# Moving column sums and gate logits into the matrix multiplications, and transposing on chip instead of through DRAM, in a fused forward and backward kernel

## The chip, the cores and the metric

The kernel runs on one core of a Trainium2 chip. The metric is the device time of one execution, in microseconds (us). The engines are named as the profile names them: PE (TensorE, matrix multiplications), PEld (its weight loads), DVE (VectorE), ACT (ScalarE), POOL (GpSimd) and SP (SyncE, which here only issues DMA transfers; "SPq" is its queue). PEclk is the clock that PE was granted, as a share of full speed. Time counts from the start of the profiled span.

A run is fast unless it is over 1.5% above the fastest run of the same kernel.

## The reference

Forward and all gradients of a gated mix of linear attention and an MLP, in bf16, with S = 2048 rows, D = 640, 32 heads of 20, and F = 1728.

```python
x = A_x                                                # (S, D)
g = sigmoid((x * gate_w).sum(-1, keepdims=True))       # one gate per row
q, k, v = split_heads(x @ wqkv)
phi = lambda t: where(t > 0, t + 1, exp(t)) + 1e-6
pq, pk = phi(q), phi(k)
kv  = einsum("bhsd,bhse->bhde", pk, v)                 # per head, over all rows
z   = einsum("bhsd->bhd", pk)                          # column sum of pk
num = einsum("bhqd,bhde->bhqe", pq, kv)
den = einsum("bhqd,bhd->bhq", pq, z)[..., None] + 1e-6
a = merge_heads(num / den) @ wo
b = relu(x @ w1) @ w2
out = g * a + (1 - g) * b       # and the gradients for x, wqkv, wo, w1, w2, gate_w
```

The kernel never forms v for all rows. It computes Y = xᵀ·pk (640 x 640), from it the head blocks KVT = wvᵀ·Y masked to a block diagonal, and from those M = KVT·wo, so that the attention output is pq·M.

## The kernel before

All stages stand in one program. For each of the 16 chunks of 128 rows, the k stage forms `kp = x_chunk @ wk` on PE and turns it into `pk` by a chain: an exponential on ACT, a tensor_scalar on DVE, a maximum on DVE. GpSimd adds every `pk` chunk into `zacc`.

```python
    def phi_chain(ps_flat, dst):
        eb = tmp("tb", 8)
        nc.scalar.activation(eb[:], ps_flat, ACT.Exp)
        cp = tmp("tb", 8)
        nc.vector.tensor_scalar(cp[:], eb[:], 1.0, 1e-6, ALU.min, ALU.add)          # L373
        nc.vector.scalar_tensor_tensor(dst, ps_flat, 1.0 + 1e-6, cp[:], ALU.add, ALU.max)   # L374

    def k_chunk(i):
        kp = pp("kp")
        for k in range(KD):
            mm_cols(kp, xT(i, k), lambda a, e: wk_s[:, k, a:e], k == 0, k == KD - 1)
        phi_chain(flat(kp)[:, 0:D], pkN[:, i, :])
        if i == 1:
            nc.gpsimd.tensor_tensor(zacc, pkN[:, 0, :], pkN[:, 1, :], ALU.add)
        elif i > 1:
            nc.gpsimd.tensor_tensor(zacc, zacc, pkN[:, i, :], ALU.add)              # L418
        ...
    nc.gpsimd.memset(KVT_s, 0.0)                                                    # L444
```

Then Y follows, five blocks of 16 x 2 matmuls. Each block needs all 16 `pk` chunks. Between the blocks stand the 16 gate products on DVE, and the fp32 column sum on PE.

```python
    for m in range(KD):
        yp = pp("yp")
        for i in range(NT):
            mm_cols(yp, xN[:, i, csl(m)], lambda a, e: pkN[:, i, a:e], i == 0, i == NT - 1)
        copy_out(m, Y_s[:, m, :], flat(yp)[:, 0:D])            # ACT for even m, DVE for odd
        for i in range(4 * m, min(4 * m + 4, NT)):
            jk = tmp("tb", 8)
            nc.vector.scalar_tensor_tensor(jk[:], xN[:, i, :], 1.0, gwb[:], ALU.mult, ALU.mult,
                                           accum_out=lg_t[:, i:i + 1])              # L454
        if m == 1:
            zp = pp("zp")
            mm_cols(zp, ones_f[:], lambda a, e: zacc[:, a:e], True, True)
            nc.scalar.copy(zb[:], flat(zp)[:, 0:D])
        ...
    nc.sync.dma_start(Y_d.rearrange("(k p) d -> p k d", p=P), Y_s)
    ...
    q_main(0)
    blockdiag(KVT_s, wv_s, Y_s)
    nc.scalar.dma_start(KVT_d..., KVT_s)
    h_half(0, 0); h_half(0, 1)
    for t in range(KD):
        ...                                                    # MT, five blocks
    nc.scalar.dma_start(MT_d..., MT_s)
    load_T(M_s, MT_d)                                          # M comes back transposed
    q_post(0)
    for i in range(1, NT + LAG):
        ...                                                    # q, h, output chunks
```

Buffers are placed by lifetime in one memory plan. `ar.add(name, bytes, t0, t1)` says from when to when a buffer lives; two buffers whose lifetimes do not overlap may share space. KVT has the lifetime `T_FF - 20` to `T_FF + 30`, so its memset must wait until the buffer whose space it takes has been read for the last time.

The order in which each engine executes is fixed when the program is built, by a scheduler that starts from the order of the code. It can move instructions that do not depend on each other.

## Time and profile before

The median of the first five runs was 652.08 us (651.24 to 652.99). These are lines of the profile's page for the kernel before: the span, the busy time of each engine (with its share of the span and its instructions), and PE's granted clock in 40 equal slices of 16 us, in tenths of full speed.

```profile
span 650.1 us, 10572 instructions
...
PE 639.2 (98%) x4480; PEld 356.8 (55%) x4480; DVE 262.2 (40%) x518; ACT 151.0 (23%) x209; POOL 119.5 (18%) x111
...
PEclk9989999999999999999999999999999999999999
```

PE is the limit: it is busy for 639.2 of 650.1 us. One slice has a lowered clock, the third (32.5 to 48.8 us). The next view names what PE waited for: the waits of PE in the kernel before, with the tile and line that waited, the releaser, and the us in total, times, and longest.

```profile
PE yp L328 <- DVE arena L374: 4.1, 1, 4.1
...
PE kp L328 <- DVE arena L374: 0.6, 1, 0.6
PE op L328 <- DMA arena<-arena: 0.6, 1, 0.6
...
```

The largest wait is one: Y's matmuls waited 4.1 us for the DVE line L374, the maximum that completes `pk`. The timeline of PE in the kernel before shows where (start, us, then engine, line, operation and count; in brackets the idle time before and its releaser).

```profile
30.70 4.24 PE L328 MATMUL yp<-arena 128*128 128x512 bf16 x30
39.01 6.46 PE L328 MATMUL yp<-arena 128*128 128x512 bf16 x34 [4.08 <-DVE arena L374]
45.30 1.30 PE L328 MATMUL zp<-arena,ones_f 128*128 128x512 f32 x4
```

Thirty matmuls ran, which is 15 of the 16 chunks; the last two of the block waited from 34.93 to 39.01. The same moments on DVE and on GpSimd, again from the timeline of the kernel before:

```profile
32.96 3.33 DVE L373 TENSOR_SCALAR tb<-tb 128x640 bf16<-128x640 bf16 x1
36.21 2.00 DVE L454 SCALAR_TENSOR_TENSOR tb<-arena,gwb 128x640 bf16<-128x640 bf16 x1
...
38.15 0.81 DVE L374 SCALAR_TENSOR_TENSOR arena<-kp,tb 128x640 bf16<-128x640 f32 x1
```

```profile
30.53 2.88 POOL L418 TENSOR_TENSOR arena<-arena 128x640 f32<-128x640 f32 x2
33.35 2.76 POOL L444 MEMSET arena<- 128x3200 bf16 x1
36.07 1.46 POOL L418 TENSOR_TENSOR arena<-arena 128x640 f32<-128x640 f32 x1
```

The last tensor_scalar took 3.33 us and ended as GpSimd's memset of KVT ended. Earlier in the k stage each tensor_scalar took 0.63 beside the sums, 0.33 without one, so that a chunk cost DVE 1.48 us and PE only 1.36.

The stall had a second cost. The windows view of the kernel before gives the busy time of PE, PEld, DVE, ACT and POOL in each stretch, then PE's clock, the share of DMA and its GB/s:

```profile
34.90:39.00 4.10, 0.04 (x1) 0.00 (x0) 4.10 (x5) 0.00 (x0) 2.63 (x2) 1.00 1.07 344
39.00:42.50 3.50, 3.49 (x13) 1.64 (x13) 3.50 (x7) 0.69 (x1) 1.84 (x1) 0.51 1.06 388
42.50:46.00 3.50, 3.50 (x24) 2.03 (x23) 3.50 (x9) 0.00 (x0) 0.00 (x0) 1.00 1.06 394
```

After the idle 4.1 us PE had half its clock: 13 matmuls in 3.5 us, then 24 in the next 3.5 us. The first two blocks of Y took 14.6 us in all, two later ones 8.7.

### The profile page before, as it was taken

How to read it: one execution, taken by the hardware profiler on the slowest of the kernel's cores; microseconds unless marked ns; L12 is line 12 of the kernel's file. 1: busy time of each engine (PE TensorE's matmuls, PEld its weight loads, DVE VectorE, ACT ScalarE, POOL GpSimd, SP SyncE). 2: the span in 40 equal slices, each digit the busy share in tenths (PEclk: the TensorE clock that was granted, in tenths of full speed). 3: DMA queues.
4: the chain of work that ended last, by engine and by line, in shares of the span. 5: the costliest groups of instructions: out<-in, count | busy, mean ns of one | idle time of the engine just before them, and what ended most of it. 6: DMA issues, size and time to landing. Idle time of an engine off the chain costs nothing.

```text
span 650.1 us, 10572 instructions
## 1 busy us (share of the span) xinstructions
PE 639.2 (98%) x4480; PEld 356.8 (55%) x4480; DVE 262.2 (40%) x518; ACT 151.0 (23%) x209; POOL 119.5 (18%) x111
## 2 busy tenths in 40 slices
PE   8979999999999999999999999999999999999998
PEld 5546555555555555555555555555555555555554
DVE  4994644554445235566135332220036320004442
ACT  4401322212222123323134343441110111110000
POOL 5840533343333213323001000000000000000000
PEclk9989999999999999999999999999999999999999
DMA  9992994645335893671749999696127539991111
GB/s 270 324 341 92 249 186 93 138 108 109 86 71 118 180 244 93 155 175 71 168 110 240 249 232 241 139 254 159 47 90 149 141 104 266 240 252 41 41 41 41
DMA packets 224889, 103.18 MB, mean 159 GB/s; under 512 B 181579, under 2 KB 224139, under 8 KB 224843
## 3 DMA queue, kind: packets, MB, share of 16 engines
q1 hardware_dynamic: 212874, 87.77, 58.0%
q10 hardware_dynamic: 11968, 14.75, 6.6%
q8 instruction: 35, 0.57, 0.4%
q14 instruction: 12, 0.09, 0.0%
HBM read 27.61 MB, written 29.66 MB: 88 GB/s over the span
## 4 chain that ended last, share of the span: by engine, by line
PE 90%; DVE 5%; DMA 2%; issue 1%; SPq 1%; ACT 1%; POOL 0%; DVEq 0%; ACTq 0%
PE op L328 11%; PE dxp L328 9%; PE gp L705 9%; PE w1p L792 9%; PE w2p L328 9%; PE dp L328 9%; PE hp L516 7%; PE rp L328 3%; PE wkp L328 3%; PE dkp L328 3%; PE qp L328 3%; PE yp L328 3%; PE xp L688 3%; PE wqp L880 3%; DVE tb L373 2%; DVE arena L374 2%
## 5 line engine op out<-in xcount | busy, mean ns | idle before, releaser
L328 PEld LDWEIGHTS <-arena 128*128 128x128 bf16 x2818 | 218.6, 98 | 175.4 <-issue 9.2
L328 PE MATMUL op<-arena 128*128 128x512 bf16 x576 | 80.9, 299 | 0.7 <-DMA arena<-arena 0.6
L516 PE MATMUL hp<-arena 128*128 128x432 bf16 x320 | 62.0, 346 | 0.0
L328 PE MATMUL dxp<-arena 128*128 128x512 bf16 x450 | 61.5, 299 | 0.0
L705 PE MATMUL gp<-arena 128*128 128x432 bf16 x320 | 60.9, 346 | 0.0
L792 PE MATMUL w1p<-arena 128*128 128x432 bf16 x320 | 60.1, 346 | 0.0
L328 PE MATMUL dp<-arena 128*128 128x512 bf16 (+1 forms) x416 | 59.6, 299 | 0.0
L328 PE MATMUL w2p<-arena 128*128 128x512 bf16 (+1 forms) x416 | 59.3, 299 | 0.0
L712 DVE TENSOR_TENSOR arena<-tb,tb 128x864 bf16<-128x864 bf16 x32 | 19.4, 607 | 65.8 <-ACT tb L709 65.7
L792 PEld LDWEIGHTS <-arena 128*128 128x128 bf16 x320 | 30.8, 98 | 26.9 <-issue 0.5
L705 PEld LDWEIGHTS <-arena 128*128 128x128 bf16 x320 | 30.5, 98 | 26.7 <-issue 1.3
L516 PEld LDWEIGHTS <-arena 128*128 128x128 bf16 x320 | 30.4, 98 | 25.8
L484 POOL TENSOR_TENSOR f<-tb,zb 128x640 f32<-128x640 bf16 x16 | 23.4, 1465 | 84.8 <-DVE tb L374 61.7
L709 ACT ACTIVATE tb<-gp,omg_t 128x864 bf16<-128x864 f32 x32 | 31.4, 981 | 32.3 <-PE gp L705 32.3
L552 DVE SCALAR_TENSOR_TENSOR tb<-op,arena 128x640 bf16<-128x640 f32 x16 | 13.2, 824 | 46.4 <-ACT arena L550 46.4
L607 POOL TENSOR_TENSOR f<-zb,grd 128x640 f32<-128x640 bf16 x16 | 20.3, 1272 | 59.4 <-DVE grd L605 59.4
L550 ACT CAST arena<-op 128x640 bf16<-128x640 f32 x16 | 11.1, 692 | 82.4 <-PE op L530 48.9
L893 DVE SCALAR_TENSOR_TENSOR f<-gwb,dl_t,arena 128x640 f32<-128x640 bf16 x16 | 14.0, 884 | 35.9 <-DMA arena<-dxB_d 35.5
L328 PE MATMUL yp<-arena 128*128 128x512 bf16 (+1 forms) x160 | 24.1, 313 | 4.1 <-DVE arena L374 4.1
L903 DVE TENSOR_TENSOR arena<-dxp,f 128x640 bf16<-128x640 f32 x15 | 12.4, 824 | 37.0 <-PE dxp L328 37.0
L373 DVE TENSOR_SCALAR tb<-tb 128x640 bf16<-128x640 bf16 x32 | 18.5, 579 | 18.8 <-ACT tb L371 18.8
L795 ACT CAST arena<-w1p 128x864 bf16<-128x864 f32 x10 | 8.8, 879 | 72.5 <-PE w1p L792 72.5
(129 smaller groups left out, 678.7 us busy)
## 6 DMA issues: line engine op xcount, KB each, us to landing
out_dram<-arena ACTq DMA_DIRECT2D x28, 160.0 KB, 3.9
pk_d<-arena SPq DMA_DIRECT2D x4, 640.0 KB, 9.5
arena<-in_grad_out_dram SPq DMA_DIRECT2D x4, 640.0 KB, 5.3
e_d<-arena SPq DMA_DIRECT2D x8, 320.0 KB, 3.5
out_dram<-arena ACTq DMA_DIRECT2D x8, 320.0 KB, 2.6
arena<-e_d SPq DMA_DIRECT2D x8, 320.0 KB, 3.7
dq_d<-arena SPq DMA_DIRECT2D x8, 320.0 KB, 4.1
dxB_d<-arena ACTq DMA_DIRECT2D x8, 320.0 KB, 3.6
```

Source lines behind the costliest of these rows:

```text
L328: mm = nc.tensor.matmul(ps_tile[:, b, 0:e - a], lhsT=lhsT, rhs=rhs_fn(a, e), start=start, stop=stop, **kw)
L373: nc.vector.tensor_scalar(cp[:], eb[:], 1.0, 1e-6, ALU.min, ALU.add)
L484: nc.gpsimd.tensor_tensor(tz[:], pq[:], zb[:], ALU.mult)
L516: nc.tensor.matmul(hp[:, nb, 0:NBW], lhsT=xT(i, k), rhs=w1_s[:, k, blk * NBW:(blk + 1) * NBW], start=(k == 0), stop=(k == KD - 1))
L607: nc.gpsimd.tensor_tensor(heads(wz[:]), heads(zb[:]), hb(w32[:]), ALU.mult)
L688: nc.tensor.matmul(xp[:, 0, :], lhsT=lhsT, rhs=doX(i)[:, 0:512], start=(i == 0), stop=(i == NT - 1))
L705: nc.tensor.matmul(gp[:, nb, 0:NBW], lhsT=doTg[i // G][:, k, gsl(i)], rhs=w2T_s[:, k, blk * NBW:(blk + 1) * NBW], start=(k == 0), stop=(k ...
L709: nc.scalar.activation(gs[:], gp[:, :, 0:NBW], ACT.Copy, scale=omg_t[:, i:i + 1])
L712: nc.vector.tensor_tensor(hs(i)[:, rng], msk[:], gs[:].rearrange("p b c -> p (b c)"), ALU.mult)
L792: nc.tensor.matmul(wp[:, nb, 0:NBW], lhsT=xN2[:, i, csl(m)], rhs=hs(i)[:, blk * NBW:(blk + 1) * NBW], start=(i == 0), stop=(i == NT - 1))
L880: nc.tensor.matmul(wp[:, 0, :], lhsT=lhsT, rhs=dqN[:, i, 0:512], start=(i == 0), stop=(i == NT - 1))
L893: nc.vector.scalar_tensor_tensor(base[:], gwb[:], dl_t[:, i:i + 1], dxB[:, i, :], ALU.mult, ALU.add)
```

## The change

Its intent is to take work off DVE and GpSimd in the k stage, to fill the end of that stage with other work of PE, and to replace trips through DRAM by transposes from on-chip memory to on-chip memory. It has eight parts:

1. The GpSimd sums `zacc` go. A column of ones is appended to x, so that each Y block (now computed as pkᵀ·x) also yields its part of the column sum z.
2. The 16 gate products on DVE go. gate_w is appended to wk as a column, so the k stage yields the logits, with one small exponential per chunk on ACT.
3. Y is computed transposed, copied by ACT, and transposed by DMA block by block. M comes back by five small transposes. The store of MT to DRAM and the transposed reloads of Y and MT from there go.
4. One of four groups of x is transposed on PE instead of two; the others come by transposing DMA.
5. The q projections of chunks 0 and 1 stand between the k stage and Y.
6. The lifetime of KVT starts at 0, so its memset need not wait.
7. Loads are reordered: gate ahead of wk, wq ahead of wv, grad_out after the first half of h(0).
8. After Y, the halves of h(0) and h(1) stand around the column sum, the block diagonal and M. For the backward pass, Y is stored to DRAM as it was computed (transposed) and loaded back plainly.

The diff, cut to its core:

```diff
-    ar.add("zacc", D * 4, 0, T_FF - 5)
-    ar.add("KVT", KD * D * B2, T_FF - 20, T_FF + 30)
+    ar.add("KVT", KD * D * B2, 0, T_FF + 30)
-    XPE = 2
+    XPE = 1
 ...
+    nc.scalar.dma_start(grow[:], gate_w.rearrange("(k p) -> k p", p=P))
     (loads of wk)
+    nc.gpsimd.memset(xN[:, :, D:D + 1], 1.0)
+    nc.tensor.transpose(gtp0[:, 0, 0:KD], grow[:], ident[:KD, :KD])
+    nc.scalar.copy(wk_s[:, :, D:D + 1], gtp0[:, 0, 0:KD].unsqueeze(2))
 ...
     def k_chunk(i):
-            mm_cols(kp, xT(i, k), lambda a, e: wk_s[:, k, a:e], k == 0, k == KD - 1)
+            mm_cols(kp, xT(i, k), lambda a, e: wk_s[:, k, a:e], k == 0, k == KD - 1, spl=DSP1)
         phi_chain(flat(kp)[:, 0:D], pkN[:, i, :])
-        if i == 1:
-            nc.gpsimd.tensor_tensor(zacc, pkN[:, 0, :], pkN[:, 1, :], ALU.add)
-        elif i > 1:
-            nc.gpsimd.tensor_tensor(zacc, zacc, pkN[:, i, :], ALU.add)
+        nc.scalar.activation(rg_t[:, i:i + 1], flat(kp)[:, D:D + 1], ACT.Exp, scale=-1.0)
 ...
+    q_main(0)
+    q_main(1)
     for m in range(KD):
         yp = pp("yp")
         for i in range(NT):
-            mm_cols(yp, xN[:, i, csl(m)], lambda a, e: pkN[:, i, a:e], i == 0, i == NT - 1)
-        copy_out(m, Y_s[:, m, :], flat(yp)[:, 0:D])
-        for i in range(4 * m, min(4 * m + 4, NT)):
-            ...gate product on VectorE...
-        if m == 1:
-            mm_cols(zp, ones_f[:], lambda a, e: zacc[:, a:e], True, True)
+            mm_cols(yp, pkN[:, i, csl(m)], lambda a, e: xN[:, i, a:e], i == 0, i == NT - 1, spl=DSP1)
+        nc.scalar.copy(YT0_s[:, m, :], flat(yp)[:, 0:D])
+        nc.vector.tensor_copy(zc_t[:, m:m + 1], flat(yp)[:, D:D + 1])
+        nc.vector.tensor_scalar(zd[:, csl(m)], ident[:], zc_t[:, m:m + 1], None, ALU.mult)
+        load_T(Y_s[:, :, csl(m)], YT0_s[:, m, :])
-    nc.sync.dma_start(Y_d..., Y_s)
+    h_half(0, 0)
+    mm_cols(zp, ones_sq[:], lambda a, e: zd[:, a:e], True, True)
+    q_den(0); q_den(1)
+    h_half(0, 1)
     blockdiag(KVT_s, wv_s, Y_s)
+    q_post(0)
+    h_half(1, 0)
     for t in range(KD):
         ...
         copy_out(t, MT_s[:, t, :], flat(mp)[:, 0:D])
-    nc.scalar.dma_start(MT_d..., MT_s)
-    load_T(M_s, MT_d)
+        load_T(M_s[:, :, csl(t)], MT_s[:, t, :])
+    h_half(1, 1)
+    q_post(1)
```

## The prediction

> **What bounds it now.** TensorE: the page shows PE busy 639.2 of 650.1 us. By the waits view its idle time lies in the first 90 us: 1.3 (first memset), 0.7 (x landing), 0.6 and 4.1 (VectorE, k stage), 0.25 and 0.6+0.3 (near the first output chunk). Later it never waits, and no later matmul is removed.
>
> **The k stage and Y.** In the PE timeline a k chunk costs 1.36 us, but VectorE needs 1.48: 0.82 for the maximum, 0.63 for the tensor_scalar, which takes 0.33 where GpSimd rests. The slow ones coincide with the 1.4 us GpSimd sums (zacc); one took 3.3 us beside the GpSimd memset of KVT. [...] Y stops for 4.08 us at its last row block, and the clock record then shows 0.5 for 3.4 us (39.1 to 42.5) [...]. The first two Y blocks take 14.6 us where two others take 8.7.
>
> **What the change removes (estimates from these durations).**
> - stall and cold clock: 14.6 - 8.7 = 5.9 us; VectorE should need about 1.2 per chunk, and two q chunks (2 x 1.36) cover its tail;
> - kp slip: 110 matmuls took 15.75, ideal 15.0: 0.75 us;
> - four of eight x transposes on PE, 0.28 each: 1.1 us;
> - the fp32 column sum (1.13) becomes bf16 (0.27): 0.85 us;
> - the DRAM round trips of Y and M. SP waited 2.2 us for MT's store, with h(1)'s transpose behind it; the first output chunks lost 1.5 us against their later pace: 1.0 to 1.5 us, if the five small transposes (1.2 us of issue each) do not block instead;
> - 16 gate products on VectorE (0.81 each): off the path, 0.
>
> Sum 9.6 to 10.1.
>
> **What it adds.** One column in 160 matmuls (under 0.1 us); a gate load ahead of wk (0.3 to 0.5 at the start); an exponential of about 0.2 per chunk on ScalarE, which has 0.65 spare. x groups 1 to 3 now come by transpose: the two of before moved 1.3 MB in about 7.3 us, so three land by about 9, 13, 17 us, needed at 13, 18, 24; wq by 24, needed at 29. The last Y block must be copied (0.7) and transposed (2.6 to 4.6) before blockdiag; PE has h(0) and the column sum, 3.9 us, to cover it: 0 to 1.5 of stall. The KVT memset moves earlier: up to 0.5. grad_out is issued behind two stores: covered by spare PSUM.
>
> Net gain 8.3 us, nearly all on the critical path: 652.1 - 8.3 = 643.8 us, 8 in 10 between 641.0 and 648.0. Faster by over 2% (below 639.0) 0.04, within 2% 0.94, slower 0.02.
>
> **What would show it.** Right: no PE wait on VectorE before Y, no 0.5 in the clock record after 5 us, kp at 1.36 per chunk, Y ending near 54 us instead of 60, the first output chunk near 71 instead of 79.5, everything later shifted as a block. Wrong: a PE wait on DMA at kp of chunk 4 or 8, at qp, or at blockdiag.
>
> **What would make it wrong.** Transposes slower than estimated among 2 MB of copies; the in-order SP queue blocked [...], so that Y's transposes start late; the scheduler placing memsets or q's phi ahead of the last k's phi.

## The result and the profile after

The kernel after took 644.56 us in the median (8 runs, 644.01 to 644.87), the kernel before beside it 652.6 us (15 runs, 651.24 to 653.93). The ratio is 0.9879, with a 95% interval of 0.9869 to 0.9889. Ratios here are the mean time of one kernel's fast runs over that of the other's of the same rounds, so not quite the ratio of the medians quoted. The gain is 8.0 us; 8.3 were predicted, and 643.8 us with a range of 641.0 to 648.0.

The same lines of the page, for the kernel after:

```profile
span 643.0 us, 10523 instructions
...
PE 636.9 (99%) x4459; PEld 355.4 (55%) x4459; DVE 240.4 (37%) x491; ACT 153.2 (24%) x225; POOL 97.9 (15%) x97
...
PEclk9999999999999999999999999999999999999999
```

The dent in the third slice is gone. PE's waits in the kernel after:

```profile
PE warm L392 <- DVE arena L379: 1.3, 1, 1.3
PE hp L507 <- DVE arena L336: 0.8, 1, 0.8
PE mtp L352 <- DVE arena L368: 0.4, 1, 0.4
PE kp L329 <- DMA arena<-in_A_wqkv_dram: 0.4, 1, 0.4
PE op L523 <- DMA arena<-arena: 0.3, 1, 0.3
```

The wait of Y is gone, and there are two new waits on DVE, 0.8 and 0.4 us, that the kernel before did not have. The timeline of DVE at the end of the k stage, kernel after:

```profile
30.72 0.33 DVE L374 TENSOR_SCALAR tb<-tb 128x640 bf16<-128x640 bf16 x1
31.15 0.82 DVE L375 SCALAR_TENSOR_TENSOR arena<-kp,tb 128x640 bf16<-128x640 f32 x1
```

This last tensor_scalar takes 0.33 us, and the last maximum ends at 31.97, before Y starts at 32.44. The timeline of PE, kernel after:

```profile
29.72 2.88 PE L329 MATMUL qp<-arena 128*128 128x512 bf16 x20
32.44 13.24 PE L329 MATMUL yp<-arena 128*128 128x512 bf16 x96
46.02 8.89 PE L329 MATMUL yp<-arena 128*128 128x512 bf16 x64
...
62.63 2.42 PE L352 MATMUL mtp<-arena 128*128 128x140 bf16 x35 [0.41 <-DVE arena L368]
65.83 1.99 PE L507 MATMUL hp<-arena 128*128 128x432 bf16 x10 [0.77 <-DVE arena L336]
```

Y runs through. The small waits come after it, at M and at h(1). PE's timelines give a full account of the 7.1 us between the two profiled spans (each figure is a difference of start times of two stages):

| stretch of PE | before, us | after, us | difference | predicted |
|---|---|---|---|---|
| start to the end of the k stage | 30.70 | 29.72 | -0.98 | -1.35 to -1.55 |
| Y without the column sum | 28.16 | 22.31 | -5.85 | -5.9 |
| column sum | 1.13 | 0.27 | -0.86 | -0.85 |
| Y to q(3), without q(0), q(1) and the column sum | 23.07 | 23.64 | +0.57 | -1.0 to -1.5 |

From q(3) on, at 85.78 us before and 78.66 after, the two kernels do the same in the same time. The timed gain is 0.9 us larger than that of the profiles, because a profile is one execution. The one of before took 652.17 us, less than that kernel's mean; the one of after took 644.83, more than its mean. The profile of before had one stretch at half clock; by their mean clocks most other runs of that kernel had two (the table under e3).

### The profile page after: what moved, and what is told of

Its sections match the earlier page's. It is cut to its first block, busy times and chain, and to the rows that moved or that the text cites. A ratio compares the mean times of both kernels' runs of the same rounds, so it can differ in the third digit from the quotient of the medians.

```text
span 643.0 us, 10523 instructions
## 1 busy us (share of the span) xinstructions
PE 636.9 (99%) x4459; PEld 355.4 (55%) x4459; DVE 240.4 (37%) x491; ACT 153.2 (24%) x225; POOL 97.9 (15%) x97
## 4 chain that ended last, share of the span: by engine, by line
PE 91%; issue 4%; DMA 2%; DVE 1%; ACT 1%; POOL 0%; ACTq 0%; POOLq 0%; DVEq 0%
PE op L329 11%; PE dxp L329 10%; PE gp L729 9%; PE w1p L816 9%; PE w2p L329 9%; PE dp L329 9%; PE hp L507 8%; PE rp L329 3%; PE wkp L329 3%; PE dkp L329 3%; PE kp L329 3%; PE qp L329 3%; PE xp L712 3%; PE wqp L904 3%; DMA arena<-in_A_wqkv_dram 1%
## 5 line engine op out<-in xcount | busy, mean ns | idle before, releaser
L800 DVE TENSOR_TENSOR tb<-dkp,dzb 128x640 bf16<-128x640 f32 x16 | 13.1, 819 | 62.5 <-PE dkp L329 62.5
L329 PE MATMUL rp<-arena 128*128 128x512 bf16 (+1 forms) x160 | 24.4, 299 | 0.0
L482 POOL TENSOR_TENSOR arena<-tb,grd 128x640 bf16<-128x640 bf16 x16 | 20.3, 1271 | 25.9 <-DVE grd L476 23.7
```

Source lines behind the costliest of these rows:

```text
L329: mm = nc.tensor.matmul(ps_tile[:, b, 0:e - a], lhsT=lhsT, rhs=rhs_fn(a, e), start=start, stop=stop, **kw)
L482: nc.gpsimd.tensor_tensor(heads(pg), heads(pq[:]), hb(grd[:]), ALU.mult)
```

## The experiments

Twelve kernels ran. This is what the letters in the expectations stand for.

- A: the stall is made at the very end of DVE's queue, by the memset beside the last tensor_scalar and by the gate product ahead of the last maximum.
- B: the stall is made by the slow pace of DVE through the whole k stage, which is due to the GpSimd sums. This is what the prediction held.
- C: the two q chunks ahead of Y are the cover that removes it.
- D: in the new kernel it is the early place of the memset that counts.

The twelve ran in three batches, each on one chip, with runs of the kernel before beside them: medians 652.78 (e), 652.29 (f) and 652.72 (g).

| run | base | edit | median us | ratio to before | correct |
|---|---|---|---|---|---|
| e1 | before | KVT's lifetime from 0 | 646.29 | 0.9903 | yes |
| e2 | before | no sums | 646.75 | 0.991 | no |
| e3 | before | no gate products | 649.1 | 0.9943 | no |
| e4 | before | q(0), q(1) ahead of Y | 657.07 | 1.0049 | yes |
| g4 | before | e1 and e3 together | 644.52 | 0.9873 | no |
| f1 | after | q(0), q(1) behind Y | 644.09 | 0.987 | yes |
| f2 | after | the sums put back, unused | 645.5 | 0.9894 | yes |
| f3 | after | KVT's lifetime as before | 644.44 | 0.9878 | yes, edit had no effect |
| g1 | after | the memset held back | 644.4 | 0.9869 | yes |
| g3 | after | masks ahead of reductions | 644.09 | 0.9875 | yes |
| f4 | after | waits after Y removed | 642.53 | 0.9846 | yes |
| g2 | f4 | gate load behind wk | 645.46 | 0.9889 | yes |

### e1: the memset early, in the kernel before

```diff
-    ar.add("KVT", KD * D * B2, T_FF - 20, T_FF + 30)
+    ar.add("KVT", KD * D * B2, 0, T_FF + 30)
```

> The kernel before with one edit: the buffer KVT may be cleared from the start, so GpSimd's 2.76 us memset no longer falls beside the last k chunk. Theory A (the 4.1 us stall was made at the end of VectorE's queue, by this memset, by a gate product placed in front of the last maximum and by the lag): last tensor_scalar 0.6 us instead of 3.3, last maximum ends near 36.4 instead of 39.0, PE stall about 1.5 us, no half clock, time lower by about 4.3 us (ratio 0.9935). Theory B (the stall was made by the 14 GpSimd sums slowing every chunk to 1.48 us, as the prediction put it): the stall stays within 1 us of what it was, time lower by at most 1 us (ratio over 0.998).

Measured: 0.9903 (0.9889 to 0.9918), 6.3 us less than before. The timeline of DVE at the end of the k stage, in e1:

```profile
33.02 0.63 DVE L373 TENSOR_SCALAR tb<-tb 128x640 bf16<-128x640 bf16 x1
33.58 2.05 DVE L454 SCALAR_TENSOR_TENSOR tb<-arena,gwb 128x640 bf16<-128x640 bf16 x1
...
35.56 0.81 DVE L374 SCALAR_TENSOR_TENSOR arena<-kp,tb 128x640 bf16<-128x640 f32 x1
36.30 0.81 DVE L454 SCALAR_TENSOR_TENSOR tb<-arena,gwb 128x640 bf16<-128x640 bf16 x1
```

The last tensor_scalar fell from 3.33 to 0.63 us, so the 2.7 us were the memset's. The gate product in front of the maximum still took 2.05 us. The next one, which began in a pause between two GpSimd sums (34.95 to 36.52), took 0.81. PE's wait at Y fell to 1.4 us, and no run of e1 had a half clock. The first two Y blocks fell from 14.61 to 10.26 us.

This accounts for 4.35 us. More came from a place that the edit does not name. The waits of the first output chunks were gone: from h(2) to q(3) PE took 9.01 us instead of 10.65. Against that, about 0.5 us was lost much later, where PE waited 0.7 us for KVT, so that the profiled spans differ by 5.5. The timed gain of 6.3 is larger because most runs of the kernel before had two stretches at half clock and its profile one (see e3). Between 55 and 80 us SP issued one load of grad_out in e1 and three in the kernel before, ahead of the transposes that those chunks need. The new memory plan had moved the loads. That this order is the cause was read from SP's timeline and not isolated by a run. One thing it does show: M's trip through DRAM was still there in e1, and PE lost nothing to it.

### e2: no sums, in the kernel before

```diff
-        elif i > 1:
-            nc.gpsimd.tensor_tensor(zacc, zacc, pkN[:, i, :], ALU.add)
```

> The kernel before without 14 of the 15 GpSimd sums (the column sum z is wrong on purpose). Theory B: VectorE follows at 1.36 us per chunk, no slip, no stall, time lower by 6.5 us (ratio 0.990). Theory A: no slip (0.75 us), but the memset still falls beside the last tensor_scalar and a gate product still stands before the last maximum: a stall of about 1.4 us without half clock stays, time lower by about 5 us (ratio 0.9923).

Measured: 0.991 (0.9894 to 0.9926) by its five fast runs, about 5.9 us less than before. That lies between what A and B gave, so the time decides nothing. Its one profile fell in a slow state (738.49 us, granted clock 0.851), so its time and PE's durations are not used. The five fast runs had mean clocks of 0.999 and 1.0, so none had a half-clock stretch. That suggests that the sums' absence alone keeps the stall short; no fast profile of e2 shows the wait itself.

The slow profile still shows the order of work on GpSimd and DVE, whose instructions took what they take in the fast profiles (tensor_scalar 0.33 us, maximum 0.82, memset 2.77). The timelines of GpSimd and DVE in e2:

```profile
33.05 2.77 POOL L442 MEMSET arena<- 128x3200 bf16 x1 [19.78 <-PE kp L328]
```

```profile
33.81 2.18 DVE L373 TENSOR_SCALAR tb<-tb 128x640 bf16<-128x640 bf16 x1 [0.33 <-ACT tb L371]
35.91 0.81 DVE L452 SCALAR_TENSOR_TENSOR tb<-arena,gwb 128x640 bf16<-128x640 bf16 x1
...
36.65 0.81 DVE L374 SCALAR_TENSOR_TENSOR arena<-kp,tb 128x640 bf16<-128x640 f32 x1
```

The memset started as the last k matmul ended (33.04). In the kernel before it started 2.5 us after that moment (33.35 against 30.86), behind sums still queued on GpSimd. The gate product took 0.81 us instead of 2.00. The last maximum ended 4.58 us after Y's start, against 8.26 in the kernel before. As an estimate: at full clock Y reaches its last chunk 4.24 us after its start, so about 0.3 us of the stall would be left. The sums thus made the stall long less by their pace than by delaying the memset (2.5 us) and lengthening the gate product (1.2).

### e3: no gate products, in the kernel before

```diff
-        for i in range(4 * m, min(4 * m + 4, NT)):
-            ...gate product on VectorE...
+        if m == 0:
+            nc.vector.memset(lg_t[:], 0.0)
```

> The kernel before without the 16 gate products on VectorE (the logits are set to 0, outputs wrong on purpose). The prediction gave them 0. Theory B: time the same within 0.5 us. Theory A: the last maximum no longer stands behind a gate product of 2.0 us, ends near 37.0, the stall is about 2.2 us [...], time lower by about 3.6 us (ratio 0.9945).

Measured: 0.9943 (0.9928 to 0.9958), 3.7 us less than before. PE's wait at Y fell from 4.1 to 2.3 us. The profile still showed a half clock behind it, so 2.3 us of idling was followed by one in this execution. The windows view of e3, with the columns as above:

```profile
37.05:40.40 3.35, 3.11 (x12) 1.44 (x12) 0.18 (x1) 0.69 (x1) 1.90 (x2) 0.50 1.08 357
```

The profiled spans differ by only 2.2 us where the timed means differ by 3.7. The mean granted clock of each run accounts for it. The clock record in the trace of the kernel before has one stretch at half clock, 3.41 us long (39.10 to 42.51), in a run with a mean of 0.997. Such a stretch takes 0.0026 off the mean of 650 us, so 0.997 is read as one, 0.995 as two, and 1.0 or 0.999 as none. Only the profiled runs show where the stretch lay; the rest is inferred:

```
kernel   mean clock of its runs                         mean time at each
before   0.997 in 10 of 27 runs, 0.995 in 17            651.9 and 653.1 us
e3       1.0 in 4 of 6 runs, 0.997 in 2                 648.6 and 649.9 us
e1       1.0 in 5 of 5 runs                             646.4 us
```

The profile of e3 is one of the two runs with a half clock. Like for like, at 0.997, the means differ by 2.0 us, as the profiles do. So the same stall costs a cold stretch in some executions only: by these clocks, 4.1 us of idling always did, for one stretch or two, 2.3 us did in two runs of six, and 1.4 us (e1) in none of five.

### g4: the memset early and no gate products, in the kernel before

The edit is e1's and e3's together.

> The kernel before with the memset early and without the gate products (outputs wrong on purpose), the 14 GpSimd sums still there. Theory A: the 1.4 us of stall that stayed with the early memset alone goes too, since the last maximum is ready near 34.5 and needed at 34.8: 1.0 to 1.5 us faster than with the early memset alone, ratio 0.988. Theory B (the sums keep VectorE behind): a stall of over 1 us stays, ratio 0.990 or more.

Measured: 0.9873 (0.9858 to 0.9887), 8.1 us less than before: the time of the whole change. The timelines of DVE and PE in g4:

```profile
33.05 0.63 DVE L373 TENSOR_SCALAR tb<-tb 128x640 bf16<-128x640 bf16 x1
33.79 0.82 DVE L374 SCALAR_TENSOR_TENSOR arena<-kp,tb 128x640 bf16<-128x640 f32 x1
```

```profile
30.81 8.86 PE L328 MATMUL yp<-arena 128*128 128x512 bf16 x63
```

The sums are still there, each tensor_scalar still takes 0.63 us, and Y does not wait. So the slow pace is not enough for the stall. It is not harmless either: the last maximum ends at 34.61 in g4, and Y's last chunk begins about 34.9, so there are 0.3 us of room. On top of this pace came 2.7 us of memset and 1.9 of gate product, together 4.6 less 0.3: about the 4.1 us of the stall.

The equal total is partly a coincidence. Like e1, g4 also lost the waits of the first output chunks (21.3 us from Y to q(3), counted as in the table above, against 23.07). g4 keeps the extra PE work that the change removes, and it lacks the waits that the change has after Y.

### e4: the q chunks ahead of Y, in the kernel before

```diff
+    q_main(0)
+    q_main(1)
     for m in range(KD):
         yp = pp("yp")
 ...
-    q_main(0)
+    q_den(0)
+    q_den(1)
```

> The kernel before with only the order changed: the first two q chunks go ahead of Y, GpSimd's sums and the memset stay. Theory C (any 2.7 us of matmuls ahead of Y suffices, what GpSimd and VectorE do does not matter): no stall, time lower by 5.8 us (ratio 0.991), the same as most of the whole change. Theory B (VectorE's lag also delays what follows): a stall of over 1 us remains. Theory A agrees with C here, because the scheduler then also places the gate products behind the last maximum: last maximum near 37.0, needed at 37.5.

Measured: 1.0049 (1.0025 to 1.0074), slower than before by 3.2 us, with runs between 653.15 and 657.66. The wait on the maximum was gone, but these came in its place (the waits of PE in e4):

```profile
PE yp L328 <- DVE arena L335: 3.3, 1, 3.3
PE op L328 <- DMA arena<-arena: 2.0, 1, 2.0
```

In DVE's queue gate products stood ahead of the copy of the second Y block, two of them at 2.0 us beside GpSimd, and PE waited for the accumulator that this copy frees. A half clock followed for 6.8 us. Theory C falls for the kernel before: the order alone moves the stall. Whether the order pays once the gate products are off DVE was not tried in this kernel; in the kernel after it did not (f1).

### f1: the q chunks behind Y, in the kernel after

```diff
-    q_main(0)
-    q_main(1)
     for m in range(KD):
 ...
+    q_main(0)
+    q_main(1)
     h_half(0, 0)
```

> The changed kernel with only the order undone: the two q chunks come after Y again. With no sums and no gate products VectorE's last maximum of the k stage should end near 32, and Y needs it near 33.8. Theory A (the stall came from the GpSimd memset and the gate product at the end of VectorE's queue): no stall, the same time as the changed kernel within 0.7 us (ratio to before 0.987 to 0.989). Theory C (the q chunks cover the stall): a stall of about 2.7 us returns, with or without half clock, 2.7 to 4.4 us slower than the changed kernel (ratio 0.992 to 0.995).

Measured: 0.987 (0.9847 to 0.9893), 644.09 us, no different from the kernel after. No wait at Y: its last maximum ended at 31.17, 2 us ahead of need. So in the new kernel the cover by q, which the prediction counted on, is not needed.

### f2: the sums back, in the kernel after

```diff
+        if i == 1:
+            nc.gpsimd.tensor_tensor(zacc, pkN[:, 0, :], pkN[:, 1, :], ALU.add)
+        elif i > 1:
+            nc.gpsimd.tensor_tensor(zacc, zacc, pkN[:, i, :], ALU.add)
```

> The changed kernel with the 15 GpSimd sums put back beside it, their result unused (outputs right). Theory B (the sums made the stall): VectorE at 1.48 us per chunk, a stall at Y returns, 4 us or more slower than the changed kernel (ratio over 0.994). Theory A: tensor_scalar 0.63 instead of 0.33, PE slips 0.5 to 0.8 us in the k stage through its PSUM buffers, no stall at Y since the last maximum is not needed before 36.5 us: 0.5 to 0.9 us slower (ratio near 0.989).

Measured: 0.9894 (0.9874 to 0.9914), 645.5 us, about 1 us more than the kernel after. Its profile showed the tensor_scalar at 0.63 us again, the k stage (150 matmuls) at 20.90 instead of 20.44, and no wait at Y. The slower pace cost 0.46 us in the k stage; where the other half of the 1 us lies was not found. The q chunks cover the end of the k stage here, so the run does not show what the sums would do without that cover.

### f3 and g1: the memset late, in the kernel after

f3 set the lifetime of KVT back:

```diff
-    ar.add("KVT", KD * D * B2, 0, T_FF + 30)
+    ar.add("KVT", KD * D * B2, T_FF - 20, T_FF + 30)
```

> The changed kernel with KVT's buffer cleared as late as before. Theory D (moving the memset is the gain, as it was when done alone): 4 to 6 us slower than the changed kernel (ratio 0.994 or more). Theory A: the last tensor_scalar is held up to 2.8 us, but no gate product follows it and two q chunks stand ahead of Y, so the last maximum (at or before 34.5) comes before it is needed (36.5): within 0.5 us of the changed kernel (ratio 0.988). The order of DMA issues differs from the changed kernel's, too, which may move the stretch after Y by up to 1 us either way.

This run tells nothing of the memset. It still ran at 6.63 us, so in the new memory plan it did not have to wait for an earlier buffer. With 644.44 us it is a repeat of the kernel after. g1 then tied the memset to a late chunk by data:

```diff
+    nc.gpsimd.tensor_copy(KVT_s[:, 0, 0:1], pkN[:, 13, 0:1])
     nc.gpsimd.memset(KVT_s, 0.0)
```

> The changed kernel, with the KVT memset held back for certain: GpSimd first copies one column of the 14th k chunk into KVT, then clears it, so it runs near 29.4 to 32.2 us, beside VectorE's last two chunks (the earlier attempt moved the buffer's lifetime only, and the memset ran at 6.6 us all the same). Theory D (the memset's place is the gain): 4 us or more slower than the changed kernel. Theory A: one tensor_scalar is held about 2.5 us, the last maximum ends near 34.5 instead of 32, Y needs it at 36.5: no PE wait, within 0.5 us of the changed kernel (ratio to before near 0.988).

Measured: 644.4 us, 0.9869 (0.9855 to 0.9884), no loss. The timelines of GpSimd and of DVE in g1:

```profile
28.91 2.82 POOL L449 MEMSET arena<- 128x3200 bf16 x1
```

```profile
30.07 1.84 DVE L374 TENSOR_SCALAR tb<-tb 128x640 bf16<-128x640 bf16 x1
32.02 0.82 DVE L375 SCALAR_TENSOR_TENSOR arena<-kp,tb 128x640 bf16<-128x640 f32 x1
```

The memset held a tensor_scalar until it ended at 31.7, as it did before. But the last maximum was then done by 32.8, and Y, behind the q chunks, needed it at about 36. D falls.

### f4, g3 and g2: the waits after Y

The new waits at h(1) and M come from orders in two queues. Here are the timelines of DVE and of SP's queue, kernel after:

```profile
60.20 0.82 DVE L474 TENSOR_REDUCE grd<-f 128x32 f32<-128x640 f32 x1 [4.08 <-POOL f L468]
60.94 1.11 DVE L514 TENSOR_SCALAR arena<-hp,omg_t 128x864 bf16<-128x864 f32 x1
```

```profile
62.34 11.39 SPq L319 DMA_TRANSPOSE arena<-arena  x7
```

DVE idled for 4.08 us in front of a reduction that waited for GpSimd. Behind it stood the second half of h(0), whose PE work had ended at 58.7, and the masks of the block diagonal, which M needs. SP's queue took 11.39 us to issue seven transposes, five of them M's, and h(1)'s stood behind.

g3 did one thing only: an order-only dependency puts the reductions of chunks 0 and 1 behind the last mask.

```diff
-        nc.vector.tensor_reduce(grd[:], heads(tz[:]), AX.X, ALU.add)
+        red = nc.vector.tensor_reduce(grd[:], heads(tz[:]), AX.X, ALU.add)
+        if i < 2:
+            (order-only dependency of red on the last mask of blockdiag)
```

> The changed kernel with one part of the improved version: VectorE's five masks of the block diagonal ahead of the two reductions. The waits on h(1) (0.6) and before M (0.4) should go, that after M (0.8) in part, the one at the output tail (0.6, SP's queue) should stay: 1.0 to 1.6 us faster than the changed kernel (ratio 0.986). If SP's queue made all of them: no difference.

Measured: 644.09 us, 0.9875 (0.9852 to 0.9897), no gain clear of the noise over the kernel after, where 1.0 to 1.6 us were expected. (Its longest run, 646.18, is the only one of the four with a mean clock of 0.997; the others had 1.0.) The waits on DVE were gone and the first output chunk began 2.2 us earlier (70.42 instead of 72.66). But then PE waited on transposes (the waits of PE in g3):

```profile
PE op L528 <- DMA arena<-arena: 0.8, 1, 0.8
...
PE op L329 <- DMA arena<-arena: 0.5, 1, 0.5
```

f4 had run before with that edit and two more: M comes by two transposes instead of five, and later loads of grad_out are tied to later h chunks.

```diff
+        (the edit of g3)
-            mm_cols(op, pqT[:, k, :], lambda a, e: M_s[:, k, a:e], False, ii == 1 and k == KD - 1)
+            mm_cols(op, pqT[:, k, :], lambda a, e: M_t[:, a // P:e // P, k, :], False, ii == 1 and k == KD - 1)
-        load_T(M_s[:, :, csl(t)], MT_s[:, t, :])
+        if t in (2, 4):
+            t0 = 0 if t == 2 else 3
+            nc.sync.dma_start_transpose(M_t[:, t0:t + 1, :, :]..., MT_s[:, t0:t + 1, :]...)
-        (load of grad_out, group g, ordered behind h_mm[0, 0])
+        (load of grad_out, group g, ordered behind h_mm[max(0, 4 * g - 2), 0])
```

> A version meant to beat both: the changed kernel with VectorE's masks of the block diagonal put ahead of the two reductions of the denominators, M transposed in two transfers instead of five, and the later grad_out loads issued no earlier than two row blocks ahead. If the waits of PE after Y in the changed kernel (about 0.6 on h(1), 0.4 and 0.8 around M, 0.6 at the tail of the first output chunk) come from VectorE's order and from SP's queue, they go: 1.5 to 2.3 us faster than the changed kernel (ratio 0.985). If they come from elsewhere (DMA rate), less than 0.5 us.

Measured: 642.53 us (642.34 to 642.74), 0.9846 (0.9823 to 0.9869), correct, and about 2 us less than the kernel after and than f3, its repeat in the same batch (644.44). It beats both kernels. Which of the edits beyond g3's matters was not separated. All of PE's waits that the view lists for f4:

```profile
PE warm L395 <- DVE arena L382: 1.3, 1, 1.3
PE gp L738 <- ACT arena L791: 0.2, 1, 0.2
```

The stretch from Y to q(3), counted as in the table above, took 21.40 us, against 23.64 in the kernel after and 23.07 in that before. M's two transposes held SP's queue for 1.94 and 1.35 us.

g2 tried to win the 0.4 us that the k stage of the kernel after waits for wk. It puts the small gate load behind the loads of wk, in f4 (whose own profile, it turned out, has no such wait):

```diff
-    nc.scalar.dma_start(grow[:], gate_w.rearrange("(k p) -> k p", p=P))
     nc.scalar.dma_start(wk_s[:, 0:2, 0:D], ...)
     nc.scalar.dma_start(wk_s[:, 2:5, 0:D], ...)
+    nc.scalar.dma_start(grow[:], gate_w.rearrange("(k p) -> k p", p=P))
```

> The version with the waits removed, with the small gate load issued behind the two wk loads instead of ahead of them. If the start waits for wk because its issue is 0.6 us later, the k stage starts 0.3 to 0.5 us earlier (ratio 0.984); if wk is late because of the transfers that share the queues, no difference within 0.2 us.

Measured: 645.46 us, 0.9889 (0.9873 to 0.9904), 3 us slower than f4. The timeline of PE in g2:

```profile
7.51 0.18 PE L397 MATMUL gtp<-ident,grow 5*128 5x5 bf16 x1 [2.23 <-DMA grow<-in_gate_w_dram]
```

The load of 1.3 KB moved only with the end of the 800 KB in front of it (by the packet records, at 6.0 to 6.4 us, and wk's last packet at 6.5; issued first, it moved at 1.8), and PE, in order, waited for it. In that profile PE then had its full clock only from 13.19 us, where the other thirteen profiles of this case had it between 4.0 and 7.3. The gate load belongs where the change put it.

## Why the prediction was right, and where it was wrong

**Right.** The total is right, 8.0 us against 8.3, and so are the terms that make most of it.

- The stall and the cold clock: 5.9 us predicted, 5.85 measured.
- The column sum: 0.85 predicted, 0.86 measured.
- Y ended at 54.75 (54 predicted), there was no wait on DVE before Y, a k chunk took 20.44 / 15 = 1.36 us as predicted, and the rest of the program shifted as a block.
- The transposed x landed in time: no wait on it is in the view.

**Mis-sized: the term of the DRAM round trips of Y and M.** The prediction gave "1.0 to 1.5 us, if the five small transposes (1.2 us of issue each) do not block instead". The stretch after Y lost 0.57 us instead. Against f4, which has hardly any wait there (21.40 us), PE's timelines split it as follows.

| place | before, us lost | after, us lost |
|---|---|---|
| ahead of M | 0 | 0.58 |
| between M's matmuls and h(1)'s second half | 0 | 1.03 |
| ahead of and within the first output chunk | 0.74 + 0.26 | 0 |
| last parts of the first two output chunks | 0.65 | 0.64 |

The waits ahead of and within the first output chunk did go, 1.00 us, as predicted. The wait at the last parts stayed, and 1.6 us came anew. The round trip as such was not what cost them, though: e1 and g4 keep M's store and transposed reload and took 21.3 us for this stretch, as little as f4. With another order of the loads around it the round trip cost PE nothing. That this order is the cause was not isolated. The prediction's proviso named the issue of small transposes, and that does keep SP's queue full (the 0.64). The larger part was not named at all: the new order let a reduction that waited for GpSimd hold up DVE's queue. g3 shows that clearing DVE alone hands the wait to SP, so both had to be known to size this term. f4 shows that clearing both gives 2 us. For the same reason the first output chunk began at 72.66 us, where about 71 was predicted (70.63 in f4).

**Mis-sized: the start.** To the end of the k stage 1.35 to 1.55 us were expected net and 0.98 came. The gate load ahead of wk was priced at 0.3 to 0.5; PE waited 0.4 us for wk. By the packet records of the traces, wk's last packet moved at 6.8 to 7.7 us in the seven profiles with the gate load ahead and at 6.4 to 6.7 in the seven others, so the load does delay wk; the wait itself varies (none in f4, which has the gate load ahead, and 0.4 in g4, which has not). And in this profile the full clock came 2.3 us later (7.26 against 4.96). As this moment varied between 4.0 and 7.3 us among profiles, that part belongs to the execution and not to the change. The forecast of "no 0.5 in the clock record after 5 us" failed in the letter for the same reason; from 7.26 on it held.

**Wrong in its reasons: what made the stall.** The prediction put the stall down to DVE's pace beside the sums, noted the memset as one slow instruction, and priced the gate products as "off the path, 0". Three delays stood in one queue ahead of the last maximum: the pace, 2.7 us of memset (e1) and 1.9 us of one gate product (e1 still shows it at 2.05 us). The sums did matter, as the prediction held, but by another way than the pace: they kept the memset back and lengthened the gate product (e2). Removing all gate products alone was worth 3.7 us (e3). Removing memset and gate products ends the stall with the sums still there (g4); removing the sums alone, with memset and gate products in place, ends the cold clock too (e2, by the clocks of its runs). So the stall had no single cause. The prediction's size was right because the change removes all three, and any reading of the cause that removes enough of them gives the same number.

**In part luck: the closeness of the totals.** The two profiles differ by 7.1 us, not 8.0. The terms of the start and of the stretch after Y fell short by about 0.5 and 1.6 to 2.1 us. What made up for it were the prediction's allowances for stalls that did not come (up to 1.5 at the block diagonal, up to 0.5 for the memset), and the second half-clock stretch that most runs of the kernel before had and that the prediction did not count.

**The parts do not add.** Against the kernel before, e1 gave 6.3 us, e2 5.9, e3 3.7, e4 lost 3.2, and all of them with the rest of the change gave 8.0. In the kernel after, the order of q (f1) and the place of the memset (g1) are worth nothing any more. A part can be worth much alone and nothing beside the others.

**Open.** How much of e1's gain beyond the stall is due to the order of the grad_out loads was not isolated. Nor was it for the stretch after Y of the kernel before. g2's 3 us beyond f4 are split between the wait of 2.23 us and the cold start only by its one profile, its slowest run (646.64 us).

## What to carry to other kernels

When the limiting engine waits once at the end of a stage, walk back through the whole queue of the engine that released it, and name every instruction in front of the last producer: an initialisation, or work that nobody needs yet, costs as much there as a slow pace does (here 2.7 us of a memset and 1.9 us of a gate product). Count an idle stretch of PE together with the half-speed stretch that can follow it (here 3.41 us, after 2.3 us of idling in two runs of six), and compare the granted clocks of runs before comparing a single profile with timed means. When you replace a few large transfers by many small ones, price the issuing queue as an engine with its own order (here 1.2 us for each small transpose), and clear all the queues that stand in front of a consumer at once, since clearing one may only move the wait (here g3 gained nothing clear of the noise, f4 about 2 us).

## What these runs measured of the engines and queues

- Half clock after idling: 2.3 us of idling led to a stretch at half clock in two of six runs (e3), 4.1 us in all of 27 runs of the kernel before, for one stretch in 10 of them and two in 17 by their mean clocks, and 1.4 us in none of five (e1). The stretch in the trace of the kernel before was 3.41 us long. Except in the profiled runs, that the stretch followed this idling is inferred. One stretch more cost about 1.2 us of the total.
- The moment of the first full clock: among thirteen profiles whose matmuls all began at about 1.3 us it came between 4.0 and 7.3 us (4.96 in the kernel before, 7.26 in the kernel after), and at 13.19 us in g2, where PE waited 2.23 us early on.
- Issue of small transposes: one of 128 x 640 held SP's queue for 1.2 us and landed after about 2.6 (kernel after); seven in a row, five of them M's, held it for 11.39 us. M in two transfers held it for 1.94 and 1.35 us (f4).
- DVE beside GpSimd: beside a GpSimd sum of 1.4 us a DVE tensor_scalar took 0.63 us instead of 0.33, and beside a sum the gate product, whose two inputs are bf16, took 2.00 to 2.05 us instead of 0.81. A memset of 128 x 3200 bf16, 2.76 us long, held a tensor_scalar until about 0.2 us after its own end: 3.33 us in the kernel before, 1.84 in g1. In the kernel before that tensor_scalar had started by the profile at 32.96, beside a sum and ahead of the memset (33.35), and it still ended after the memset.
- A small load queued behind large ones: one of 1.3 KB behind 800 KB on the same queue moved at 6.0 to 6.4 us and made PE wait until 7.51 (g2); issued first, it moved at 1.8 (kernel after).
